# Order of the vector sums where upper products follow each other, and of the last batch's first lower products, in a fused attention and SwiGLU kernel

## The chip, the core and the metric

The kernel runs on one core of a Trainium2 chip. The time is the device time of one execution in microseconds, the median of three runs. The profile is of one execution; its span is a little shorter than the device time, and times "at 857.02" are microseconds from the start of that span. TensorE (PE in the profile, PEld for its loads of weights) multiplies matrices, VectorE (DVE) and ScalarE (ACT) do elementwise work, GpSimd (POOL) and SyncE (SP) mostly start transfers.

## What is computed

Two stages. The first is attention in which a query sees only keys of the same hash bucket; the second is a SwiGLU feed-forward block on its output, with the heads side by side (4 batches x 768 rows, 512 wide; d_ff is 1536). Cut to what matters:

```python
mask = q_bucket[:, :, :, None] == k_bucket[:, :, None, :]
scores = np.where(mask, scale * np.matmul(q, k.transpose(0, 1, 3, 2)), -1e9)
attn = softmax(scores)                      # with 1e-9 in the denominator
attn_out = np.matmul(attn, v)               # (4, 8, 768, 64)

x = attn_out.transpose(0, 2, 1, 3).reshape(3072, 512)
g = x @ w_gate                              # 512 -> 1536
silu = g * (1.0 / (1.0 + np.exp(-g)))
val = x @ w_val
out = (silu * val) @ w_out                  # 1536 -> 512
```

All of it is in fp32.

## The kernel before

The feed-forward block is done batch by batch while the attention of later batches goes on. Its "upper" part is the two products with `w_gate` and `w_val`, its "lower" part the product with `w_out`. Both use Strassen's scheme in Winograd's form: of two by two blocks, seven products instead of eight, at the price of sums of blocks before and after. Sums are made on VectorE (`plus`, line 597), the products by `product` (line 593).

The upper part of a batch is six groups (`both(i)`), each of which makes the gate and the value for two blocks of hidden columns. From the second batch on, two of the seven products of a group are split once more (`deeper`), which needs four more sums of weight blocks, r3, r2, r1, r4, made by `weigh`. A group is a list of ten steps; each step becomes an "atom", and the atoms of all work not yet done stand in one list.

```python
def look_ahead():
    if atoms:
        finish(getattr(atoms[0][1], "ahead", []))

def up_strassen(x, b, first):
    ...
    def both(i):
        ...
        def weigh(d):
            _, block, *_, rs, _ = deep[d]
            v11, v12, v21, v22, r1, r2, r3, r4 = inner_weights(block, rs)
            for o, p, q, op in ((r3, v11, v21, ALU.subtract), (r2, v22, r3, ALU.subtract),
                                (r1, r2, v11, ALU.add), (r4, v12, r2, ALU.subtract)):
                plus(o, p, q, op)
        ...
        if nested:
            order = (0, 2, 4, 1, 5)
        todo = [[lambda at, n=n, g=g: outer(n, g, at)] for n in order for g in range(2)]
        if nested:
            for d, at in ((0, 2), (1, 6)):
                for go in range(4):
                    todo[at + go].insert(0, lambda at, d=d, go=go: deeper(d, go, at))
                if d:
                    todo[at - 1].insert(0, lambda at, d=d: weigh(d))
        ahead = [lambda: weigh(0)] if nested else []

        def step(at):
            if at == 0:
                while first:
                    first.pop(0)()
                finish(ahead)
            for do in todo[at]:
                do(at)
            if at == len(todo) - 1:
                look_ahead()
                settle(at + NB)
        ...
        begin.ahead = ahead
```

`finish` empties a list by calling what is in it, so `weigh(0)` of a group runs once: at the last step of the group before it if `look_ahead` finds it there, else at the group's own first step. `settle` runs what is left of the gating (line 571, which reads a tanh that ScalarE makes in the one buffer `th`, and line 575). `deeper(0, 0)`, in step 2, is the first to use r1.

The lower part of a batch is three chunks of seven products, each of six matmuls, into the banks a, b and c; what is added to a bank is copied out by ScalarE (line 811) or added by VectorE in between:

```python
def down_strassen(out_of):
    ...
    def combine(i, which, part):       # half of the sums of hidden blocks of chunk i
        ...                            # 1: s1 = a21 + a22;  2: s2 = s1 - a11;
                                       # 3: a21 = a11 - a21 (s3);  4: s4 = a12 - s2
    def chunk(i):
        now = {}

        def step(n):
            a11, a12, s3, a22 = parts(i, slice(None))
            if n == 0 and i == 0:
                while next(preparing, None):
                    pass
                for which in (1, 2, 3):
                    combine(0, which, 1)
            ...
            a, w, to = ((a11, b11, "a"), (s1, t1, "b"), (s2, t2, "a"), (a12, b21, "c"),
                        (s3, t3, "a"), (s4, b22, "b"), (a22, t4, "a"))[n]
            c = now[to]
            product(c, [(a[:, f], w[:, f]) for f in range(NFP)], n in (0, 1, 3))
            r, x = ((0, 0), (1, 1), (0, 1), (0, 0), (1, 1), (0, 1), (1, 0))[n]
            o = now["o"][r][x]
            if n in (3, 4, 5):
                plus(o, o, c)
            else:
                nc.scalar.copy(o, c)
            ...
    ...
    return lambda: [combine(0, which, 0) for which in (1, 2, 3)]

def push_ffn(b):
    ...
    up_strassen(x, b, first)
    at = len(atoms) - 1
    early = down_strassen(out_of)
    size, last, end = atoms[at]
    atoms[at] = (size, lambda: (early(), last()), end)
```

`early` makes the first half of the lower part's first sums; `last` is the last step of the upper part. The main loop goes over the attention's units (scores, line 494; exponentials on ScalarE, line 497; their product with v, line 509) and takes some atoms off the list after each; what is left when the attention is done is run at the end:

```python
for u in range(0, N, NCH):
    ...
    while atoms and (credit > 0 or not end):
        size, atom, end = atoms.pop(0)
        credit -= size
        atom()
        ...
for _, atom, _ in atoms:
    atom()
```

Of the kernel before, what the change touches and what calls it, by code (L numbers as in the profile page):

```python
# [18 lines left out]
def kernel(  # L19
# [13 lines left out]
    B, H, S, D = q.shape  # L33
# [3 lines left out]
    CH = NCH // 2  # L37
# [31 lines left out]
    def bank(name):  # L69
        return banks.tile([P, 512], FP32, tag="ps", name=name)  # L70
# [124 lines left out]
    NB = 7  # L195
# [67 lines left out]
    def as_words(t):  # L263
        return t.bitcast(I32).rearrange("p (f w) -> p f w", w=2)

    spots = [hid[:, half, m].rearrange("p f q -> p (f q)") for half in range(2) for m in range(2)]
    early = [as_words(t[:, 0 : 2 * PIECE]) for t in spots]
# [117 lines left out]
    atoms = []  # L385
# [143 lines left out]
    def total(n):  # L529

        b, pr = pairs[n]

        ps = av_ps.tile([P, 512], FP32, tag="av", name="sum") if b == 0 else bank("sum")
        t = [acc.pop((n, half)) for half in range(2)]
        for h in range(2):
            for half in range(2):
                g = (2 * h + half) * BLOCK
                nc.tensor.matmul(ps[g : g + BLOCK, 0:HQ], ones, t[half][:, h, :],  # L540
                                 start=True, stop=True)
        if b == 0:
            space = wo.rearrange("p f m -> p (f m)")
            space = space[:, n % 2 * 3 * HQ : (n % 2 + 1) * 3 * HQ].rearrange("p (x q) -> p x q", q=HQ)
            r, t = space[:, 2, :], space[:, 0:2, :]
        else:
            r, t = t[1][:, 0, :], t[0]
        nc.vector.reciprocal(r, ps[:, 0:HQ])
        for half in range(2):
            for h in range(2):  # L550
                g = (2 * h + half) * BLOCK
                for at in (h * D, h * D + BLOCK):
                    nc.sync.dma_start(t[at : at + BLOCK, half, :], r[g : g + BLOCK, :])
        waiting.append(lambda: norm(n, t))
        if pr == NP - 1:
            push_ffn(b)
# [33 lines left out]
    def product(ps, pairs_, start):  # L590

        for i, (a, x) in enumerate(pairs_):
            nc.tensor.matmul(ps, a, x, start=start and i == 0, stop=i == len(pairs_) - 1,  # L593
                             skip_group_check=True)

    def plus(o, a, b, op=ALU.add):
        nc.vector.tensor_tensor(o, a, b, op=op)  # L597
# [162 lines left out]
        for i in range(NG // 2):  # L760
            both(i)

    def down_strassen(out_of):


        t2, t3, t4 = down_t
        t1 = b12
        s2, s1, s4 = down_s

        def parts(i, fs):  # L770
            return [hid[:, half, m, fs, i * P : (i + 1) * P]
                    for half in range(2) for m in range(2)]

        def combine(i, which, part):
            fs = slice(part * NFP // 2, (part + 1) * NFP // 2)
            a11, a12, a21, a22 = parts(i, fs)
            if which == 1:
                plus(s1[:, fs], a21, a22)
            elif which == 2:
                plus(s2[:, fs], s1[:, fs], a11, ALU.subtract)  # L780
            elif which == 3:
                plus(a21, a11, a21, ALU.subtract)
            else:
                plus(s4[:, fs], a12, s2[:, fs], ALU.subtract)

        def chunk(i):
            now = {}

            def step(n):
                a11, a12, s3, a22 = parts(i, slice(None))  # L790
                if n == 0 and i == 0:
                    while next(preparing, None):
# [3 lines that stand above are left out]
                if n == 0:  # L796
                    for name in "cba":
                        now[name] = bank("po")[:, 0:HD]
                    o = word_room[0]
                    now["o"] = [[o[:, (2 * r + x) * HD : (2 * r + x + 1) * HD] for x in range(2)]  # L800
                                for r in range(2)]
# [10 lines that stand above are left out]
                if n >= 3:  # L812
                    nc.sync.dma_start(out_of(r, i)[:, x * HD : (x + 1) * HD], o)
                for part in range(2):
                    if n == 0:
                        combine(i, 4, part)
                    elif n in (3, 4) and i + 1 < CH:
                        for which in ((1,), (2, 3))[n - 3]:
                            combine(i + 1, which, part)

            for n in range(NB):
                atoms.append((2, lambda n=n: step(n), n == NB - 1))

        for i in range(CH):
            chunk(i)
        return lambda: [combine(0, which, 0) for which in (1, 2, 3)]

    def push_ffn(b):
        x = [xT[b, pr] for pr in range(NP)]
        rows = out[b * S : (b + 1) * S, :].rearrange("(p c) m -> p c m", c=NCH)  # L830

        def out_of(half, i):
            return rows[:, half * CH + i, :]

        up_strassen(x, b, first)
        at = len(atoms) - 1
        early = down_strassen(out_of)
        size, last, end = atoms[at]
        atoms[at] = (size, lambda: (early(), last()), end)

# [14 lines left out]
    for u in range(0, N, NCH):  # L857
        n, half, _ = units[u]
# [49 lines left out]
        end = True  # L908
        part = 0
        while atoms and (credit > 0 or not end):  # L910
            size, atom, end = atoms.pop(0)
# [11 lines left out]
            for _ in range(size):  # L923
                if chores:
                    step = chores.pop(0)
                    chores.extend(step and step() or [])
        while chores:
            step = chores.pop(0)
            chores.extend(step and step() or [])
    for _, atom, _ in atoms:  # L930
        atom()


# [30 lines left out]
```

The softmax here doesn't subtract the row's maximum and nothing guards it: scores larger than these inputs give would overflow.

## Time and profile before

| | us |
|---|---|
| time, median of 3 runs | 995.05 (994.68 to 995.08) |
| span of the profiled execution | 992.9 |
| matmuls of the upper products, L593 `up`, two largest groups of rows | 243.0 and 176.9 busy |
| matmuls of the lower products, L593 `po`, three groups of rows | 66.6, 66.9 and 66.1 busy |
| sums and gating on VectorE, all instructions | 670.4 busy |

From about 820 us on the attention is done: the last batch's six upper groups follow each other up to about 933 us, and then its three lower chunks to the end.

In a timeline each row is: start, duration, engine, line, operation, output and inputs with their shapes, and how many instructions were merged into the row. In brackets stands how long the engine was idle before it and what ended that idle time. One fp32 matmul of the code shows as two records, or passes. The matmul's end is modelled, so the distance of two starts is a better measure than the duration.

### The profile page before, as it was taken

To read this page: it belongs to the slowest core of one execution; us is meant where nothing else is said; L and a number is where in the kernel's file an instruction comes from. 1 tells how busy PE (TensorE), PEld (TensorE's weight loads), DVE (VectorE), ACT (ScalarE), POOL (GpSimd) and SP (SyncE) were. 2 spreads that over 40 slices of the span, in tenths; PEclk is the share of its full clock that TensorE was granted. 3 is DMA by queue.
4 is the path that set the end of the run, shared out by engine and by line. 5 is a ranking of instruction groups with operands and counts; after the bars stand their busy time and mean duration, and the time that the engine had idled before them with its cause. 6 is when DMAs were issued, how large, how long until landed. Compare 5 with 4: busy or idle time off the path is not lost.

```text
span 992.9 us, 13575 instructions
## 1 busy us (share of the span) xinstructions
PE 980.0 (99%) x4813; PEld 625.0 (63%) x4813; DVE 670.4 (68%) x1276; ACT 408.1 (41%) x921; POOL 127.3 (13%) x248
## 2 busy tenths in 40 slices
PE   9999999999999999999999999999999999999998
PEld 4444555555577766656566775666666786666687
DVE  5899888888965556777784457776776446667631
ACT  7999555566512234444442313443342202323200
POOL 3222232231100011111010001111100001121000
PEclk9999999999999999999999999999999999999999
DMA  8777685875303042433322114343121112233001
GB/s 235 218 249 229 157 259 178 228 269 157 106 26 76 16 121 79 104 92 84 99 81 57 52 31 108 98 107 100 57 87 33 35 34 85 75 117 105 1 30 35
DMA packets 119987, 107.02 MB, mean 108 GB/s; under 512 B 90032, under 2 KB 104848, under 8 KB 119920
## 3 DMA queue, kind: packets, MB, share of 16 engines
q0 software_dynamic: 18336, 73.29, 23.0%
q1 hardware_dynamic: 100784, 32.67, 14.2%
q8 instruction: 38, 0.62, 0.3%
q10 hardware_dynamic: 800, 0.20, 0.1%
q14 instruction: 29, 0.24, 0.1%
HBM read 81.79 MB, written 17.30 MB: 100 GB/s over the span
## 4 chain that ended last, share of the span: by engine, by line
PE 91%; DVE 5%; issue 2%; ACT 2%; POOL 0%; DMA 0%; DVEq 0%; ACTq 0%; POOLq 0%
PE up L593 41%; PE po L593 21%; PE sc L494 14%; PE av L509 11%; PE sum L540 1%; PE hps L412 1%; DVE c L571 1%; DVE hid L575 1%; PE tps L396 1%; DVE hid L597 1%; DVE room L368 0%; DVE inner L597 0%; PE idle L134 0%; DVE acc L527 0%; ACT th L570 0%
## 5 line engine op out<-in xcount | busy, mean ns | idle before, releaser
L593 PE MATMUL up<-xT,room 128*128 128x384 f32 (+1 forms) x732 | 243.0, 465 | 0.0
L593 PEld LDWEIGHTS up<-xT,room 128*128 128x128 f32 x732 | 134.8, 190 | 73.3 <-issue 9.8
L593 PE MATMUL up<-xc,room 128*128 128x384 f32 (+1 forms) x540 | 176.9, 455 | 0.0
L327 POOL DMA_DIRECT2D room<-ram x144 | 77.9, 543 | 677.8 <-PE up L593 662.4
L494 PE MATMUL sc<-qT,kT 64*128 64x384 f32 x768 | 161.0, 494 | 0.0
L597 DVE TENSOR_TENSOR c<-c,up 128x192 f32<-128x192 f32 (+1 forms) x198 | 78.9, 406 | 80.9 <-PE up L593 76.5
L527 DVE TENSOR_TENSOR acc<-acc,A 128x768 f32<-128x768 f32 x128 | 122.7, 958 | 15.7 <-ACT A L497 2.9
L593 PEld LDWEIGHTS up<-xc,room 128*128 128x128 f32 x540 | 99.2, 190 | 43.8 <-DVE c L597 1.1
L570 ACT ACTIVATE th<-c 128x384 f32<-128x384 f32 x90 | 46.9, 522 | 158.1 <-DVE c L571 89.7
L497 ACT ACTIVATE A<-sc 128x384 f32<-128x384 f32 x256 | 103.9, 528 | 0.6 <-PE sc L494 0.5
L494 PEld LDWEIGHTS sc<-qT,kT 64*128 64x128 f32 x768 | 67.9, 186 | 54.3 <-issue 40.5
L811 ACT COPY words<-po 128x256 f32<-128x256 f32 x48 | 17.9, 373 | 199.0 <-PE po L593 180.1
L597 DVE TENSOR_TENSOR hid<-hid,up 128x192 f32<-128x192 f32 (+1 forms) x162 | 67.5, 418 | 43.5 <-PE up L593 41.6
L509 PE MATMUL av<-A,vraw 128*64 128x384 f32 (+1 forms) x512 | 88.2, 486 | 0.0
L597 DVE TENSOR_TENSOR words<-words,po 128x256 f32<-128x256 f32 x36 | 15.2, 421 | 99.2 <-PE po L593 99.2
L679 ACT COPY c<-up 128x384 f32<-128x384 f32 x72 | 34.4, 478 | 88.8 <-PE up L593 88.7
L593 PE MATMUL po<-wo,room 128*128 128x256 f32 x288 | 66.6, 380 | 1.5 <-DVE room L597 1.5
L593 PE MATMUL po<-wo,hid 128*128 128x256 f32 x288 | 66.9, 382 | 0.0
L593 PE MATMUL po<-room,hid 128*128 128x256 f32 x288 | 66.1, 379 | 0.0
L509 PEld LDWEIGHTS av<-A,vraw 128*64 128x64 f32 x512 | 36.7, 137 | 46.1 <-issue 44.1
L494 PE MATMUL sc<-qb,kb 64*128 64x384 bf16 x384 | 65.1, 323 | 0.5 <-DVE kb L426 0.5
L593 PEld LDWEIGHTS po<-wo,hid 128*128 128x128 f32 x288 | 54.1, 190 | 12.1 <-issue 4.9
(137 smaller groups left out, 1165.3 us busy)
## 6 DMA issues: line engine op xcount, KB each, us to landing
room<-ram POOLq DMA_DIRECT2D x96, 384.0 KB, 3.7
vraw<-in_v_dram SPq DMA_DIRECT2D x16, 384.0 KB, 3.3
ram<-room POOLq DMA_DIRECT2D x12, 512.0 KB, 5.1
room<-ram POOLq DMA_DIRECT2D x48, 128.0 KB, 3.5
out_dram<-words SPq DMA_DIRECT2D x48, 128.0 KB, 1.7
room<-in_moe_w_out_dram POOLq DMA_DIRECT2D x10, 512.0 KB, 6.4
qraw<-in_q_dram SPq DMA_DIRECT2D x48, 96.0 KB, 3.2
hid<-in_moe_w_gate_dram POOLq DMA_DIRECT2D x9, 512.0 KB, 6.8
```

The costliest lines, as they stand in the source:

```text
L327: nc.gpsimd.dma_start(places[k % 2][:, PARTS[go], :], ram[k % NG][:, PARTS[go], :])
L396: nc.tensor.transpose(ps[:, i * P : (i + 1) * P], raws[name, n][:, half * CH + i, :, :].rearrange("p h d -> p (h d)"), ident)
L412: nc.tensor.matmul(tile_[i * BLOCK : (i + 1) * BLOCK, 0:HQ], hash_w, T[name, n][:, half * HQ : (half + 1) * HQ], start=True, stop=True)
L494: nc.tensor.matmul(sc[h], x["k", n][rows, ks], x["q", n][rows, qs], start=start, stop=not start)
L497: nc.scalar.activation(weights(u)[:, h, 0:HQ], sc[h], AF.Exp, scale=SCALE * (OFF / 2 if n <= NP else 1.0))
L509: nc.tensor.matmul(ps[h * D : (h + 1) * D, 0:width], raws["v", n][:, h, c, :], a[:, h, 0:width], start=c == 0, stop=c == NCH - 1)
L527: nc.vector.tensor_tensor(acc[n, half], acc[n, half], a[:, :, 0:HQ], op=ALU.add)
L570: nc.scalar.activation(th, g, AF.Tanh, scale=0.5)
L593: nc.tensor.matmul(ps, a, x, start=start and i == 0, stop=i == len(pairs_) - 1, skip_group_check=True)
L597: nc.vector.tensor_tensor(o, a, b, op=op)
L679: nc.scalar.copy(tile_of(g, spot), c)
L811: nc.scalar.copy(o, c)
```

## The change

Three edits, all of the order in which instructions are put into the engines' queues; none adds or removes an operation. First, the loop at the end takes each atom off the list before it runs it, so that `look_ahead` at a group's last step finds the next group and makes its `weigh(0)` there, as it does inside the main loop. Second, in the first three batches the first half of the lower sums (`early`) is put behind the last upper step instead of ahead of it; in the last batch it stays ahead. Third, the first lower chunk of the last batch, which follows its upper part at once, takes product 3 (of a12, which needs no sum) right after product 0, so that the sums for products 1 and 2 have more time.

```diff
-    def down_strassen(out_of):
+    def down_strassen(out_of, at_once):
...
         def chunk(i):
             now = {}
 
-            def step(n):
+
+            order = (0, 3, 1, 2, 4, 5, 6) if at_once and i == 0 else range(NB)
+
+            def step(at):
+                n = order[at]
                 a11, a12, s3, a22 = parts(i, slice(None))
...
-                    elif n in (3, 4) and i + 1 < CH:
-                        for which in ((1,), (2, 3))[n - 3]:
+                    elif at in (3, 4) and i + 1 < CH:
+                        for which in ((1,), (2, 3))[at - 3]:
                             combine(i + 1, which, part)
...
-        early = down_strassen(out_of)
+        early = down_strassen(out_of, b == B - 1)
         size, last, end = atoms[at]
-        atoms[at] = (size, lambda: (early(), last()), end)
+
+        atoms[at] = (size, lambda: (early(), last()) if b == B - 1 else (last(), early()), end)
...
-    for _, atom, _ in atoms:
-        atom()
+    while atoms:
+        atoms.pop(0)[1]()
```

## The prediction

> **What bounds the kernel now.** I read the page first, then the list of waits, then the timeline around the places that the diff names. Three lines of the page carry the first step.
>
> ```profile
> span 992.9 us, 13575 instructions
> PE 980.0 (99%) x4813; PEld 625.0 (63%) x4813; DVE 670.4 (68%) x1276; ACT 408.1 (41%) x921; POOL 127.3 (13%) x248
> ...
> PE 91%; DVE 5%; issue 2%; ACT 2%; POOL 0%; DMA 0%; DVEq 0%; ACTq 0%; POOLq 0%
> ```
>
> TensorE carries 91% of the chain that ended last, and its clock row reads 9 in every slice. The change adds and removes no operation, so it can only win back the stretches in which TensorE waits for another engine. The chain gives DVE and ACT 7%, which overstates it: some of those steps lie beside matmuls. The list of waits names one regular wait of the matmuls themselves: "PE up L593 <- DVE inner L597", 5.7 us, 5 times, longest 1.1. The timeline of one of the five, first TensorE's matmuls, then VectorE (start, duration, engine, line, operation, output and inputs, count, idle before and its releaser):
>
> ```profile
> 857.02 4.36 PE L593 MATMUL up<-xT,room 128*128 128x384 f32 x14
> 862.53 0.59 PE L593 MATMUL up<-xT,inner 128*128 128x192 f32 x2 [1.15 <-DVE inner L597]
> ```
>
> ```profile
> 859.46 0.55 DVE L575 SCALAR_TENSOR_TENSOR hid<-c,hid 128x384 f32<-128x384 f32 x1
> 860.13 0.56 DVE L571 SCALAR_TENSOR_TENSOR c<-th,c 128x384 f32<-128x384 f32 x1
> 860.61 1.02 DVE L575 SCALAR_TENSOR_TENSOR hid<-c,hid 128x384 f32<-128x384 f32 x2
> 861.54 0.28 DVE L597 TENSOR_TENSOR inner<-room 128x128 f32<-128x128 f32 x1
> 861.86 0.29 DVE L597 TENSOR_TENSOR inner<-room,inner 128x128 f32<-128x128 f32 x1
> 862.19 0.29 DVE L597 TENSOR_TENSOR inner<-inner,room 128x128 f32<-128x128 f32 x1
> ```
>
> TensorE has ended one group of upper products and begun the next; a weight block of its third step (r1, in `inner`, made at 862.19) is a sum that VectorE makes only after the gating of the group before. The same wait of 1.15 us stands at 843.63, 881.43, 900.33 and 919.23.
>
> **What the Trainium skill says.** "PSUM — Partial Sum Buffer", section "Engine vs sequencer instructions": VectorE and ScalarE queues are strict FIFO, and matmuls stay in program order while a weight load may run ahead. The trace agrees: the sums at 861.54 need nothing made at 860.13, yet stand behind it, and weight loads lead their matmuls by 0.16 us. So the order of the code decides. The same page, "PSUM bank collisions raise a hardware error": accesses of different engines to one bank have to be kept apart by semaphores. So a product that adds into a bank must wait until ScalarE has read it; in the kernel before, another product always lies between in the lower chunks, so its trace shows no such wait there. "Perfetto Trace Analysis", section "Identifying the Most-Contended Engine": matmul busy time is no measure of headroom. Here PE reads 99% and PEld 63%, so I size waits by the distance of starts, not by idle time.
>
> **Part 1, sums ahead at the end.** The final loop walked over the list without taking atoms off, so the look-ahead at a group's last step saw a stale head. Now it sees the next group. The order on the engines confirms five moved blocks: four sums (r3, r2, r1, r4) move ahead of one L571 and two L575. The last batch has six groups in a row, hence five seams.
>
> Worth of a seam: a group of the same shape without the wait is the first of the six.
>
> ```profile
> 821.94 3.07 PE L593 MATMUL up<-xT,room 128*128 128x384 f32 x10
> 824.84 0.49 PE L593 MATMUL up<-xT,inner 128*128 128x192 f32 x2
> ...
> 838.13 4.36 PE L593 MATMUL up<-xT,room 128*128 128x384 f32 x14
> ```
>
> The start of the last product of a group, four passes of 0.323 us (four of 128x384 take 1.29 from start to start, 825.49 to 826.78; two of 128x192 take 0.33, 824.84 to 825.17), is the start of an x14 run, so the first group lasts from 821.94 to 838.13 + 1.29 = 839.42, which is 17.48 us. The second lasts from 839.42 to 857.02 + 1.29 = 858.31, which is 18.89. The loss per seam is 1.41, not 1.15, because the modelled end of a matmul hides a part.
>
> Will r1 be in time? In the new order the four sums follow the L575 of 859.46; with VectorE's spacing of 0.47 they begin at 859.93, and the matmul can follow 0.99 after their start (862.53 - 861.54): 860.92. TensorE wants to load r1 at 857.02 + 12 x 0.323 + 0.33 - 0.16 = 861.07. Slack 0.15 us: enough, but thin. The gating then ends at about 862.45, and the plus on the first inner bank comes about 0.95 us later than in the first group; TensorE comes back to that bank 4.84 us after the group's start (863.16), by when the plus (to 862.8) is done. The blocks that r1 is made of were loaded earlier: issues at 830.80 to 832.95 with a median landing time of 3.7 us. So 5 x 1.41 = **7.0 us**.
>
> **Part 2, lower sums behind the last upper part (batches 1 to 3; the fourth keeps the old order).** The three sums of 0.56 us stood ahead of the last group's plus and gating. In the second batch, on ScalarE:
>
> ```profile
> 509.35 0.52 ACT L570 ACTIVATE th<-c 128x384 f32<-128x384 f32 x1 [2.21 <-DVE c L571]
> 509.78 1.62 ACT L497 ACTIVATE room<-sc 128x384 f32<-128x384 f32 x4
> ```
>
> They hold up the L571 that frees the single tanh buffer, so the tanh, behind it the exponentials in ScalarE's queue, and with these the banks of the scores. Scores (L494) last from 507.10 to the first row of L509 at 512.92, 5.82 us. At an ordinary group end (478.77 to 483.81) they last 5.04, with exponentials from 480.36, 1.6 us after the first score instead of 2.7. The third batch has the same, 747.54 to 753.35. In the first batch scores last 5.04 already. Gain 0.78 + 0.77 = **1.55 us**. VectorE's total stays, so it begins the row sums 0.3 to 0.5 us later; the lower product's s1 would be ready at about 518.4 and its second half is wanted at about 520.1. No new wait there.
>
> **Part 3, the last batch's first chunk.** Its order becomes 0, 3, 1, 2, 4, 5, 6.
>
> ```profile
> 936.50 1.46 PE L593 MATMUL po<-wo,room 128*128 128x256 f32 x6
> 938.95 1.56 PE L593 MATMUL po<-wo,room 128*128 128x256 f32 x6 [0.99 <-DVE room L597]
> 940.35 2.75 PE L593 MATMUL po<-room 128*128 128x256 f32 x12
> 942.94 2.75 PE L593 MATMUL po<-wo,hid 128*128 128x256 f32 x12
> ```
>
> A product takes 2.59 us (940.35 to 942.94). Product 1 starts at 936.50 and product 2 at 940.35 instead of 939.09: loss 1.26. With product 3 in between, product 1 starts at 939.09, and its late half of s1 (done 938.9) is in time. Product 3 reads a12, whose last part is gated by 938.31 and wanted at about 938.45. So 1.26 is gained. But now 4 follows 2 directly and adds into the same bank; ScalarE's copy (L811) begins 0.20 after product 2 (943.14 against 942.94) and takes 0.37, and with 0.05 to 0.1 of release (r1's release took 0.05) TensorE waits about 0.65. Net **0.6 us**.
>
> **Sum.** 7.0 + 1.55 + 0.6 = 9.15; 995.05 - 9.15 = 985.9, or 0.9%.
>
> **Rivals.** (A) VectorE takes the place of the wait at the seams: r1 misses its slack of 0.15, or the gating that now comes later holds up banks. For it: the thin slack, and the 0.95 us delay of the first plus. Against it: group ends inside the attention loop have the sums ahead already, with r1's row at 480.93, 3.55 us after the start of the group's last product (477.38), and its end at 3.84; my 860.92 is 3.90 after 857.02. Half of part 1 lost gives about 989.5. (B) The bank wait in part 3 is longer than the wait it removes, or product 3 waits for a12. Then part 3 costs up to 0.5 and the time is 987. (C) Part 2 brings nothing, because the exponentials are late for the scores' own sake, or VectorE, which was busy without a break from 505.6 to 511.4, hands the delay on to the lower chunk, as it does in the first batch (a wait of 0.49 at 280.41). Then 987.5. All of them together give about 992; none makes the kernel slower, since each part only reorders work that is small beside its stage.
>
> **Range and chances.** The five seams are alike, so they succeed or fail together; that makes the upper side longer. The runs before spread by 0.4 us. I take 984.8 to 988.5. Two per cent is 19.9 us, twice the sum of all waits that the change touches: within 2% has 0.985, faster by over 2% 0.008, slower 0.007.
>
> **What would show each step.** Right: no wait of TensorE on `inner` at the seams and five starts 17.5 us apart; scores of 5.04 us at the ends of the second and third batch's upper part; no wait on `room` in the last batch's first lower chunk, and one of about 0.65 on ScalarE before its fifth product. Wrong: a remainder on `inner` or on banks at the seams, or a wait of the lower chunks on `room` that the kernel before did not have.

## The result, and the profile after

| | before | after |
|---|---|---|
| time, us | 995.07 (994.68 to 995.16) | 986.06 (985.76 to 986.30) |
| span of the profiled execution, us | 992.9 | 983.9 |

The ratio is 0.991, with a 95% interval of 0.9893 to 0.9927: 9.0 us less, where 9.15 were forecast. The page of the changed kernel, the same rows as before:

```profile
PE 977.7 (99%) x4813; PEld 624.2 (63%) x4813; DVE 669.6 (68%) x1276; ACT 408.2 (41%) x921; POOL 127.2 (13%) x248
...
PE 95%; DVE 2%; ACT 2%; issue 1%; DVEq 0%; ACTq 0%
```

The busy times are the same to within 0.3%; what went is waiting. In the chain, DVE has fallen from 5% to 2%. The end of that chain in order of time (start, duration, engine, output, line, count) shows how few steps are left between TensorE's own:

```profile
820.76 104.89 PE up L593 x408
925.66 10.37 PE po L593 x48
936.05 0.38 ACT words L815
936.48 44.31 PE po L593 x204
```

In the kernel before, the six upper groups of the last batch were cut by DVE and ACT steps at each of five seams. Now they are one stretch of 408 matmuls, and the only step between there and the end of TensorE's work is a copy by ScalarE. (This copy, line 811 of the kernel before, is line 815 now.)

**The seams.** TensorE, then VectorE, at the first of the five:

```profile
836.79 4.36 PE L593 MATMUL up<-xT,room 128*128 128x384 f32 x14
840.99 0.49 PE L593 MATMUL up<-xT,inner 128*128 128x192 f32 x2
```

```profile
839.22 0.55 DVE L575 SCALAR_TENSOR_TENSOR hid<-c,hid 128x384 f32<-128x384 f32 x1
839.69 0.28 DVE L597 TENSOR_TENSOR inner<-room 128x128 f32<-128x128 f32 x1
840.01 0.29 DVE L597 TENSOR_TENSOR inner<-room,inner 128x128 f32<-128x128 f32 x1
840.33 0.29 DVE L597 TENSOR_TENSOR inner<-inner,room 128x128 f32<-128x128 f32 x1
840.54 0.28 DVE L597 TENSOR_TENSOR room<-room,inner 128x128 f32<-128x128 f32 x1
840.75 0.55 DVE L571 SCALAR_TENSOR_TENSOR c<-th,c 128x384 f32<-128x384 f32 x1
```

The four sums now begin 0.47 us after the L575 and the second L571 comes behind them. r1 (840.33) ends at 840.62, and its matmul starts at 840.99, 4.20 us after the x14 run, with no idle time in the brackets. The x14 runs start at 836.79, 854.27, 871.76, 889.24 and 906.72: 17.48 us apart, where it was 18.90.

**The scores in the second batch.** ScalarE around the last tanh of the upper part:

```profile
508.46 0.52 ACT L570 ACTIVATE th<-c 128x384 f32<-128x384 f32 x1 [1.12 <-DVE c L571]
508.89 1.62 ACT L497 ACTIVATE room<-sc 128x384 f32<-128x384 f32 x4
```

The tanh waits 1.12 us for the L571 instead of 2.21. TensorE's first score and its first product with v, in the kernel before and then in the changed one:

```profile
507.10 0.92 PE L494 MATMUL sc<-qT,kT 64*128 64x384 f32 x4
512.92 1.52 PE L509 MATMUL av<-room,vraw 128*64 128x386 f32 x8
```

```profile
507.30 0.92 PE L494 MATMUL sc<-qT,kT 64*128 64x384 f32 x4
512.34 1.52 PE L509 MATMUL av<-room,vraw 128*64 128x386 f32 x8
```

From one to the other it takes 5.04 us instead of 5.82. In the third batch it is 746.97 to 752.02, 5.05.

**The last batch's first lower chunk**, on TensorE:

```profile
925.49 5.34 PE L593 MATMUL po<-wo,hid 128*128 128x256 f32 x24
930.67 2.75 PE L593 MATMUL po<-wo,room 128*128 128x256 f32 x12
933.26 2.75 PE L593 MATMUL po<-room 128*128 128x256 f32 x12
936.48 2.86 PE L593 MATMUL po<-room,hid 128*128 128x256 f32 x12 [0.46 <-ACT words L815]
939.17 2.75 PE L593 MATMUL po<-wo,room 128*128 128x256 f32 x12
```

Products 0 and 3 run as one row of 24, product 1 follows without a wait on `room`. Product 4 starts 3.22 us after product 2 instead of 2.59, because it now waits for ScalarE's copy: 0.63 us. It also takes 2.69 us to the start of product 5 instead of 2.59. Its first weight load starts together with it at 936.48, where the load of product 1 was 0.21 us ahead of its matmul (930.46 against 930.67). So the new wait costs 0.73 us in all.

### The profile page after: what moved, and what is told of

Same layout as the page of the kernel before. It is cut to its first block, busy times and chain, and to the rows that moved or that the text cites. A ratio compares the mean times of both kernels' runs of the same rounds, so it can differ in the third digit from the quotient of the medians.

```text
span 983.9 us, 13575 instructions
## 1 busy us (share of the span) xinstructions
PE 977.7 (99%) x4813; PEld 624.2 (63%) x4813; DVE 669.6 (68%) x1276; ACT 408.2 (41%) x921; POOL 127.2 (13%) x248
## 4 chain that ended last, share of the span: by engine, by line
PE 95%; DVE 2%; ACT 2%; issue 1%; DVEq 0%; ACTq 0%
PE up L593 42%; PE po L593 22%; PE sc L494 15%; PE av L509 12%; PE sum L540 1%; PE hps L412 1%; PE tps L396 1%; ACT A L497 1%; ACT kb L417 1%; DVE room L368 0%; PE idle L134 0%; DVE acc L527 0%; ACT room L497 0%; DVE hid L575 0%; DVE c L571 0%
## 5 line engine op out<-in xcount | busy, mean ns | idle before, releaser
L527 DVE TENSOR_TENSOR acc<-acc,A 128x768 f32<-128x768 f32 x128 | 122.6, 958 | 15.7 <-ACT A L497 2.9
```

The source lines that it names most:

```text
L527: nc.vector.tensor_tensor(acc[n, half], acc[n, half], a[:, :, 0:HQ], op=ALU.add)
```

## The experiments

Each run was timed in alternation with the kernel before, whose median was 995.03 to 995.17 in these runs. The changed kernel (986.06) was timed on another occasion than the runs that are set against it below, so of those differences a tenth or two says nothing. The first question is whether the three parts add up.

**Part 1 alone.** The kernel before with

```diff
-    for _, atom, _ in atoms:
-        atom()
+    while atoms:
+        atoms.pop(0)[1]()
```

> The kernel before with the first edit alone (atoms taken off the list at the end, so that the four sums of the next group go ahead of the last gating). Theory: five seams of 18.89 us become 17.48, so 7.0 us less, 988.0; no wait of TensorE on inner at the seams. Rival (the parts support each other, and the seams alone give back a part through VectorE's later gating): 989 to 991.5, with a remainder on inner or on a bank.

Measured: 987.91 (987.73 to 988.23), ratio 0.9926 with an interval of 0.9912 to 0.9940, 7.1 us less than before. The x14 runs are 17.48 us apart, and no matmul of the upper products waits on `inner`. The theory holds; VectorE's later gating gives nothing back.

**Part 2 alone.** The kernel before with

```diff
-        atoms[at] = (size, lambda: (early(), last()), end)
+        atoms[at] = (size, lambda: (early(), last()) if b == B - 1 else (last(), early()), end)
```

> The kernel before with the second edit alone (first lower sums behind the last upper step in batches 1 to 3). Theory: the scores at the ends of the second and third batch's upper part take 5.04 us instead of 5.82, so 1.55 us less, 993.5. Rival (the sums are only pushed on and hold up the lower chunk or the row sums): 995.0, with a new wait on room.

Measured: 993.37 (993.21 to 994.43), ratio 0.9983 (0.9976 to 0.9990), 1.7 us less. The scores of the third batch last from 746.73 to 751.77, 5.04 us. No wait on `room` was added. The theory holds.

**Part 3 alone.** The kernel before with the order of the diff's `order` line, and the old loop and the old place of `early`.

> The kernel before with the third edit alone (order 0, 3, 1, 2, 4, 5, 6 in the last batch's first chunk). Theory: the wait on room (1.26 us from start to start) goes, a wait of 0.63 on ScalarE's copy between products 2 and 4 comes, so 0.6 us less, 994.4. Rival (the bank wait costs as much as it saves): 995.0.

Measured: 994.47 (994.24 to 994.98), ratio 0.9994 (0.9986 to 1.0002). The median is 0.56 us less, as forecast, but the interval includes no difference. The trace settles it: products 0 and 3 in one run, product 1 without a wait, and product 4 3.21 us after product 2 (944.86 against 941.65). From product 0 to product 5 it takes 13.68 us (933.88 to 947.56); before it took 14.21 (933.91 to 948.12), a difference of 0.53. That is the 1.26 us of the old wait less 0.73 for the new one (941.65 to 947.56 is 5.91 us, two products without a wait are 5.18).

The three medians add to 7.12 + 1.66 + 0.56 = 9.3 us; together they bring 9.0. The spread of each is some tenths, so they are independent as far as this can tell.

**Is the wait in part 3 one for the bank?** The changed kernel with products 1 and 2 exchanged, so that 2 and 4, which add into bank a, have product 1 between them:

```diff
-            order = (0, 3, 1, 2, 4, 5, 6) if at_once and i == 0 else range(NB)
+            order = (0, 3, 2, 1, 4, 5, 6) if at_once and i == 0 else range(NB)
```

> The changed kernel with the order 0, 3, 2, 1, 4, 5, 6 in that chunk: products 2 and 4, which add into one bank, no longer follow each other, and s2 is wanted 2.6 us earlier than in the changed kernel. Theory (the 0.63 us is the bank wait): it goes, 985.4. Rival (s2, the third sum in VectorE's queue, is late): a wait on room in its place, 986.0 or more.

TensorE in that run:

```profile
925.42 5.34 PE L593 MATMUL po<-wo,hid 128*128 128x256 f32 x24
930.60 2.75 PE L593 MATMUL po<-room 128*128 128x256 f32 x12
933.19 2.75 PE L593 MATMUL po<-wo,room 128*128 128x256 f32 x12
935.78 2.75 PE L593 MATMUL po<-room,hid 128*128 128x256 f32 x12
```

Five products in a row, each 2.59 us after the one before, and no wait. Measured: 985.13 (984.81 to 986.27), 0.9 us less than the changed kernel. One of its four runs is as long as the changed kernel's, so here the trace decides: from product 0 to product 5 it takes 12.95 us (925.42 to 938.37) instead of 13.68 (925.49 to 939.17), 0.73 less. Product 2 has its sum s2 in time although it comes 2.6 us earlier, so the exchange costs nothing. Product 4 reads the same sum s3 as before and now starts 10.36 us after product 0 instead of 10.99, so it had not been waiting for that sum. The bank was the reason.

**The same order in every batch.** In addition:

```diff
-            order = (0, 3, 2, 1, 4, 5, 6) if at_once and i == 0 else range(NB)
+            order = (0, 3, 2, 1, 4, 5, 6) if i == 0 else range(NB)
```

> The changed kernel with the order 0, 3, 2, 1, 4, 5, 6 in the first chunk of every batch. In the first batch TensorE waited for s1 there (0.48 us by the profile, 0.75 from start to start). Theory: that wait goes too, so 0.63 + 0.75 less than the changed kernel, 984.7. Rival (in the first batch VectorE is behind with other work, so s2 is late as well): 985.4.

Measured: 984.41 (984.33 to 984.67), ratio 0.9892 (0.9878 to 0.9905), 0.7 us less than the run before this one. In the first batch's first chunk the wait of 0.48 us on `room` is gone; products 2 and 1 follow at 281.05 and 283.64. From product 0 to product 4 it takes 10.47 us there (275.76 to 286.23) instead of 11.22 in the changed kernel (275.97 to 287.19), the 0.75 that was expected.

**What holds the scores in part 2: the tanh buffer or the banks?** The kernel before, in which the three lower sums of the second and third batch go behind the last two pluses on upper banks, but stay ahead of the gating:

```diff
                     c = my[spot]
+                while between and n == 5 and g == 1:
+                    between.pop()()
                 settle(at)
...
-        atoms[at] = (size, lambda: (early(), last()), end)
+        if b in (1, 2):
+            atoms[at] = (size, lambda: (between.append(early), last()), end)
+        else:
+            atoms[at] = (size, lambda: (early(), last()), end)
```

> The kernel before in which, in the second and third batch, the three lower sums go behind the last two pluses on the banks of the upper products, but still ahead of the gating that frees the tanh buffer. Theory (the exponentials wait in ScalarE's queue behind a tanh that waits for the buffer): no gain, scores still take 5.8 us or a little more, 995.0 to 996.0. Rival (the banks that those pluses free were what the scores waited for): 993.5, scores of 5.04 us.

ScalarE in the second batch:

```profile
509.98 0.52 ACT L570 ACTIVATE th<-c 128x384 f32<-128x384 f32 x1 [2.65 <-DVE c L571]
510.41 1.62 ACT L497 ACTIVATE room<-sc 128x384 f32<-128x384 f32 x4
```

Measured: 995.92 (995.62 to 996.46), ratio 1.0008 (0.9999 to 1.0016). The banks are free as early as in the changed kernel, and nothing is won: the scores take 6.27 us (507.28 to 513.55), because the tanh still waits for the L571 behind the sums, now 2.65 us, and the exponentials wait behind the tanh. VectorE's last sum into `c`, the tanh's input, had ended at 506.30, so what the tanh waits for is the buffer. That the sums stood ahead of the L571 is the cause.

**How much room has r1?** The changed kernel with r3 made twice in `weigh(0)`, the second over the first, which puts 0.32 us more of VectorE's time ahead of r1:

```diff
-                for o, p, q, op in ((r3, v11, v21, ALU.subtract), (r2, v22, r3, ALU.subtract),
+                for o, p, q, op in ((r3, v11, v21, ALU.subtract),) * (2 if d == 0 else 1) + ((r2, v22, r3, ALU.subtract),
```

> The changed kernel in which the sum r3 of weigh(0) is made twice at each group from the second batch on, the second over the first: one more VectorE sum of 128x128 in front of r1, about 0.32 us. Theory (r1 comes about 0.15 us ahead of its use at the five seams): TensorE waits 0.17 to 0.3 us at each of the five, 0.85 to 1.5 us more, 986.9 to 987.6, and a wait on inner at each seam. Rival (r1 has room to spare): 986.1 as the changed kernel.

Measured: 988.52 (988.37 to 988.83), 2.5 us more than the changed kernel; neither theory had that. At the seams the x14 runs are 17.61 us apart, only 0.13 more each. The load of r1, in the changed kernel, and the load and matmul of r1 in this run, where the x14 run starts at 838.59:

```profile
840.83 0.35 PEld L593 LDWEIGHTS up<-xT,inner 128*128 128x128 f32 x2
```

```profile
842.80 0.30 PEld L593 LDWEIGHTS up<-xT,inner 128*128 128x128 f32 x2
842.80 0.59 PE L593 MATMUL up<-xT,inner 128*128 128x192 f32 x2
```

The load starts 4.21 us after the x14 run instead of 4.04, so it is 0.17 late. Of the 0.32 us the other 0.15 was slack. The rest of the 2.5 us is in the loop. TensorE at the row sums of a unit in the third batch:

```profile
673.74 1.02 PE L540 MATMUL sum<-acc,ones 128*32 128x384 f32 x5
674.40 0.49 PE L412 MATMUL hps<-qT,hash 128*32 128x384 f32 x1
674.58 0.50 PE L540 MATMUL sum<-acc,ones 128*32 128x384 f32 x3
```

Three of the eight passes come late: they wait for the last of VectorE's additions to `acc`, and the list of waits has "PEld sum L540 <- DVE acc L527", 2.2 us, 6 times, which the changed kernel's list does not have. In the chain, the row sums and the `hps` product behind them take 1.92 us together instead of 1.59 (377.72 to 379.64, and 377.90 to 379.49 in the changed kernel). Six times this 0.33 us and five times 0.13 make 2.6 us. To separate the two, r3 was made twice at the seams alone:

```diff
-                for o, p, q, op in ((r3, v11, v21, ALU.subtract),) * (2 if d == 0 else 1) + ...
+                for o, p, q, op in ((r3, v11, v21, ALU.subtract),) * (2 if d == 0 and tail else 1) + ...
...
+    tail.append(True)
     while atoms:
         atoms.pop(0)[1]()
```

(`tail` is a list that is empty until the final loop.)

> The changed kernel with r3 made twice at the seams of the last batch alone, not inside the attention loop. Theory (at a seam r1 comes about 0.2 us before it would hold TensorE up, and most of the 2.4 us of the run with r3 twice came from six row sums in the loop that wait for VectorE): the seams become 17.61 us long instead of 17.48, 0.65 us more than the changed kernel, 986.7. Rival (the seams carry the 2.4 us): 988.5.

Measured: 986.66 (986.37 to 988.00), 0.6 us more than the changed kernel. So about three quarters of the 2.5 us came from the loop. At a seam 0.15 us more of VectorE's time would be free, and beyond that it costs.

**A gain from that.** The six row-sum products take 0.94 to 0.95 us in the chain even in the changed kernel, and 0.78 in the first batch, and at 543.85 and 783.52, where no `weigh(0)` stands in front of the additions. So the look-ahead that part 1 extends to the end is placed too early inside the loop, where scores and attention lie between two groups. The last run builds on the order in every batch:

```diff
                 if at == len(todo) - 1:
-                    look_ahead()
+                    tail and look_ahead()
...
+    tail.append(True)
     while atoms:
         atoms.pop(0)[1]()
```

Inside the loop the four sums are then made by the call of `look_ahead` that stands behind the unit's additions to `acc`.

> The kernel with the order 0, 3, 2, 1, 4, 5, 6 in every first chunk, in which the look-ahead at a group's last step acts only after the attention loop; inside the loop the four sums then go behind the unit's row sums instead of ahead of them. Theory (six row-sum products in the loop wait 0.16 us for VectorE because those four sums of 1.07 us stand in front): the product of the row sums takes 0.78 us as in the first batch instead of 0.94, about 1.0 us less, 983.4. Rival (r1 is now late for the group's third step, or nothing is won): 984.4 or more, with a wait on inner inside the loop.

VectorE's additions in the same unit, first with the order in every batch, then in this run, where the first of the four sums follows them:

```profile
483.04 4.15 DVE L527 TENSOR_TENSOR acc<-acc,A 128x768 f32<-128x768 f32 x4
```

```profile
481.96 4.14 DVE L527 TENSOR_TENSOR acc<-acc,A 128x768 f32<-128x768 f32 x4
486.02 0.28 DVE L597 TENSOR_TENSOR inner<-room 128x128 f32<-128x128 f32 x1
```

In the first the additions end at 487.19, after the row-sum product began at 487.07; in the second they end at 486.10, and the product begins at 486.72. All six products take 0.78 us in the chain. Measured: 983.31 (983.08 to 983.38), ratio 0.9881 (0.9865 to 0.9898), 1.1 us less than with the order alone and 2.75 less than the changed kernel. No matmul waits on `inner`. This is the fastest version found.

**The last batch's sums behind its upper part as well.** The changed kernel with

```diff
-        atoms[at] = (size, lambda: (early(), last()) if b == B - 1 else (last(), early()), end)
+        atoms[at] = (size, lambda: (last(), early()), end)
```

> The changed kernel with the lower sums behind the last upper step in the last batch too. Theory: with product 3 in between, the sums have 2.6 us more, and the same VectorE work lies in front of the second half of s1 in either order, so no difference, 986.1, within 0.3. Rival (the last batch needs its sums ahead, as the changed kernel keeps them): a wait on room before product 1, 986.6 to 987.5.

Measured: 986.03 (985.72 to 986.29): no difference. Product 1 starts 5.18 us after product 0 in both. The exception for the last batch, which the change makes, is not needed once product 3 stands second.

## Why the prediction was right

**Part 1** was forecast at 7.0 us and brought 7.1 alone. Both halves of the argument held. The loss per seam was to be taken from starts, 1.41 us, and not from the idle time of 1.15; the five seams are 1.42 shorter. The sums follow the L575 at VectorE's spacing, and the matmul of r1 starts with no wait; the slack of 0.15 us was real: with 0.32 us of extra work the load of r1 came 0.17 late. The prediction's reason for 1.41 against 1.15 is only a part of it. The modelled end of the x14 run (861.38) lies 0.16 us behind the place of the next matmul (857.02 + 4.20 = 861.22), and the other 0.10 is that the block after r1 followed 0.43 us later (862.53 to 862.96) instead of 0.33. The later plus on the first inner bank starts 4.07 us after its group (842.15 against 838.08), forecast 4.14, and TensorE comes back to the bank 4.84 after, as forecast. Rival A, half of it lost to VectorE, fell.

**Part 2** was forecast at 1.55 and brought 1.7 alone, and the scores' length went to 5.04 us as forecast. The chain of reasons (sums, L571, tanh buffer, exponentials, banks of the scores) was argued in the prediction and is shown by the run that freed the banks of the upper products early but not the tanh buffer. No run gave the tanh a second buffer, so that one link rests on the trace: its input is there 3.7 us before it starts. VectorE begins the row sums 0.33 us later after allowing for the 0.20 by which this trace lies behind; s1 is ready at 518.56 and its second half wanted at about 520.4. Rival C fell.

**Part 3** was forecast at 1.26 - 0.65 = 0.6 us. The wait on `room` went, and product 4 started 0.63 us late. What the sum left out is the 0.10 us by which product 4 itself then lasts longer. So the bank wait costs 0.73, and the net is 0.53. Rival B, a bank wait longer than the one removed, fell, but more than half of the gain (0.73 of 1.26) did go there, and one exchange of two products avoids it.

What the prediction did not see is that the row sums in the loop already waited for VectorE by 0.16 us, six times. It lies outside the change, so it cost the forecast nothing, but the claim that "each part only reorders work that is small beside its stage" and so cannot make the kernel slower is too strong: there, whether the four sums stand ahead of the additions decides on 0.16 us of TensorE's time, and 0.32 us more of VectorE's time ahead of them cost TensorE 0.33. The prediction took group ends inside the loop as evidence that r1 comes in time, and it does; what waits behind the four sums there it did not look at.

## What to carry to other kernels

Where one engine is busy nearly all the time, count a wait by the distance of starts against an equal stretch without the wait, and look for what stands ahead in the queue of the engine waited for: here most of the loss came from sums standing behind, or ahead of, work that they did not depend on. When products are reordered to hide one wait, see which of them add into the same accumulator, and keep another product between. A look-ahead that pays where groups follow each other can cost where other work lies between them; place it for each case.

## What the runs showed of the hardware that was not expected

Where a weight load started together with its matmul instead of ahead of it, the next weight block or product came about 0.1 us later, even where the matmul itself was hardly late. With r3 made twice, the matmul of r1 started 4.21 us after the x14 run instead of 4.20, but its load, which otherwise led by 0.16 us, started with it, the next weight block came 0.43 us later instead of 0.32, and the seam became 0.13 us longer. The same 0.10 us is found in two other places where load and matmul start together: at the seams of the kernel before (0.43 instead of 0.33) and in product 4 behind the bank wait (2.69 instead of 2.59).

ScalarE's copy of 0.37 us between two products into one bank cost TensorE 0.73 us: 0.63 to the start of the second product and 0.10 within it. The profile gives only 0.46 of it as idle.
